# Attention, expert layer and gated layer on one core: the gated layer's token chunks 408, 408 and 272 wide

## The chip, the cores and the metric

One core of one Trainium2 chip runs the whole kernel. The metric is the time of one execution on the device, in microseconds (us). Three executions of the kernel before took 453.52, 452.41 and 452.5 us, median 452.5 us.

## What is computed

Four batches of 1088 tokens go through three layers, all in float32:

```python
k_p, q_p = phi(k), phi(q)                  # phi: outer product of two 8-wide projections, per head
x = (q_p @ (k_p.T @ v)) / (q_p @ k_p.sum(0) + 1e-6)          # 1. attention, 4 heads of 32
xk, xr = mix(x, x_prev, mu_k), mix(x, x_prev, mu_r)
x = sigmoid(xr @ w_r) * (relu(xk @ w_k)**2 @ w_v)             # 2. expert layer, 128 -> 1024 -> 128
u, v = split(relu(x @ w_in))                                  # 3. gated layer, 128 -> 2 x 512
v_n = (v - mean(v)) / sqrt(var(v) + 1e-6)
v_s = w_spatial @ v_n + b_spatial          # 1088 x 1088 over the tokens, per batch
out = (u * v_s) @ w_out                                       # 512 -> 128
```

In what follows "the first part" is attention and the expert layer, which the kernel runs interleaved, and "the second layer" is the gated layer.

## The kernel before, in words

**Precision.** A float32 product is made of three matmuls on rounded halves (`mm3`, line 128: low x high, high x high, high x low). `copy` (line 133, ScalarE) makes a high half, `low` (line 137, VectorE or GpSimd) the low half.

**The first part.** Tokens are cut into the chunks of `CH` (line 22: 384, 384, 320), twelve over the four batches. `features`, `k_sum`, `q_turn`, `q_num` and `q_out` (lines 204 to 301) are attention; `up`, `sqsplit` and `down` (lines 354 to 410) step through 96 slices of the expert layer. A table `todo`, filled by `plan` (line 937), says after which slice each other piece of work is put into the program. Small buffers of this part have tags of their own: `bs0`, `bs1`, `sab` (line 215), `va0`, `va1` (line 198), `kb0`, `kb1` (line 243), `Sbd` (line 848), `de0`, `de1` (line 279). A tag is one buffer; a new tile of a tag waits until the old one is no longer used.

**The second layer, batch 0.** `spatial` (line 548) makes one unit: 128 of the 512 channels (d) times one chunk of output tokens (c). It has 3 matmuls for u, 24 for the token product (8 blocks of 128 tokens), 2 for the tail of 64 tokens and the bias, and 3 for the output product (`put_out`, line 573): 32 matmuls as wide as the chunk. The twelve units run in the order of `ORD0` (line 64); the first four, chunks 0 and 1 of d = 0 and 1, are put among the last slices of the first part (`ES`, line 49, planned at line 1010), the last four have chunk 2. The token matrix is loaded by chunk (`wload`, line 431) into two staging buffers `st0` and `st1` and split by `wconv` (line 439).

**The second layer, batches 1 to 3.** `group` (line 694) takes two of the four channel blocks, so there are six groups. Chunks 0 and 1, both 384 wide, and the two halves of 1024 tokens make a 2 x 2 block product, which is done with seven half-size products instead of eight (`prod`, line 709; sums of the token matrix in `sums`, line 639, kept at the places of `CHOME`, line 79; sums of v in `build`, line 680). A product is 4 blocks x 3 = 12 matmuls, so a group has 84 of them, 384 wide. Chunk 2, 320 wide, is done plainly: four calls of `plain` (line 714) of 12 matmuls each, 48 a group. Around these, each of a group's two channel blocks has for each chunk 3 matmuls for u (`pre`, line 698), 2 for the tail (`tmm`, line 719) and 3 for the output product.

**The order.** The program is traced in this order, and a scheduler that simulates the engines' times then orders the instructions of each engine. `behind` (line 896) pins some of them.

```python
CH = ((0, 384), (384, 384), (768, 320))                                     # line 22
ORD0 = ((0, 0), (1, 0), (0, 1), (1, 1), (2, 0), (3, 0), (2, 1), (3, 1), (3, 2), (0, 2), (1, 2), (2, 2))
```

Of the kernel before, what the change touches and what calls it, by code (L numbers as in the profile page):

```python
# [78 lines left out]
CHOME = {(1, 2): ("tt", 0), (3, 2): ("tt", 1), (1, 3): ("tt", 2), (3, 3): ("tt", 3), (1, 0): ("tt", 4), (3, 0): ("x0",),  # L79
# [5 lines left out]
def attn_moe_gmlp(ctx: ExitStack, tc: tile.TileContext, qT, kT, va, st, wk, wv, wr, win, wout,  # L85
# [118 lines left out]
    def features(src, c, dst, pb=4, eng=None, early=False):  # L204
        wide = bank(pb)
        ab = wide[:, :192].rearrange("p (t h r) -> p t h r", t=3, h=NH)
        for t in range(3):
            TE.matmul(wide[:, 64 * t:64 * t + 128], lhsT=src[:, cut(c, t, CH[c][0])], rhs=Sbd, start=True, stop=True)  # L208
        if eng is None:
            bs = sb(rot("bs0", "bs1"), [128, 3, NH, 8])  # L210
            copy(bs, ab[:, :, :, 8:16])
            a_ = ab[:, :, :, 0:8].rearrange("p t h i -> p (t h) i")
            b_ = bs.rearrange("p t h j -> p (t h) j")
        else:
            sab = sb(m(2 + c) if early else "sab", [128, 3, NH, 16])
# [52 lines left out]
    def q_num(i):  # L268
# [10 lines left out]
        den = sb(rot("de0", "de1"), [128, 3, NH])  # L279
# [138 lines left out]
    def wplace(k, c):  # L418
        if c < 2:
            t = WTAGS[NT * c + k]  # L420
            return (t, 0), (t, CMAX)
        return (WTAGS[2 * k], 2 * CMAX), (WTAGS[2 * k + 1], 2 * CMAX)

    def wtile(k, c):
        n = CH[c][1]
# [5 lines left out]
    def wload(k, c):  # L431
        o, n = CH[c]
# [6 lines left out]
    def wconv():  # L439
        k, c, src = pending_raw.pop(0)  # L440
        done.add((k, c))
        o, n = CH[c]
# [105 lines left out]
    def spatial(b, d, c, fill, early=False):  # L548
# [6 lines left out]
        o, n = CH[c]  # L555
# [17 lines left out]
    def put_out(b, d, c, g, early=False):  # L573
        o, n = CH[c]
# [21 lines left out]
    def ctile(n, k):  # L596
# [5 lines left out]
        if (n, k) not in ct:  # L602
            tags = CHOME[n, k]
            if tags[0] == "tt":
                if "c" not in xv:
                    xv["c"] = sb("tt", [128, 5, 2, CMAX], F32R)
                ct[n, k] = tuple(xv["c"][:, tags[1], x] for x in range(2))
            elif len(tags) == 1:
                t = sb(tags[0], [128, 2, CMAX], F32R)
                ct[n, k] = t[:, 0], t[:, 1]  # L610
            else:
                ct[n, k] = tuple(sb(t, [128, CMAX], F32R) for t in tags)
        return ct[n, k]

    def wraw(dst, n, k):
        o = CH[n % 10 - 1][0]
        r = 128 * (k + HALF * (n // 10 - 1))
        nc.sync.dma_start(out=dst, in_=wT[r:r + 128, o:o + CMAX])
# [75 lines left out]
    def group(b, p):  # L694
# [3 lines left out]
        def pre(d, c, relu=False):  # L698
            o, n = CH[c]
# [24 lines left out]
        def snap(acc):  # L724
            a = sb(rot(m(8), m(9), m(10), m(11)), [128, CMAX])
# [37 lines left out]
        X = bank(0)[:, :CMAX]  # L763
# [7 lines left out]
        Y = bank(1)[:, :CMAX]  # L771
# [7 lines left out]
        Y = bank(1)[:, :CMAX]  # L779
# [13 lines left out]
        Z = bank(6)[:, :CMAX]  # L793
# [15 lines left out]
        if last_group:  # L809
            while gout:  # L810
                flush()
            ob = sb(rot(m(6), m(7)), [128, CMAX])
            for h in range(2):
                cs = slice(CMAX // 2 * h, CMAX // 2 * h + CMAX // 2)
# [4 lines left out]
            nc.sync.dma_start(out=out[:, b * S + CMAX:b * S + 2 * CMAX], in_=ob)  # L819
# [341 lines left out]
```

## Time and profile before

| what | value |
|---|---|
| median of three executions | 452.5 us (452.41 to 453.52) |
| the profiled execution | 452.46 us |
| its span (first to last instruction) | 450.7 us |
| TensorE busy in the span | 440.8 us, 98% |
| VectorE, ScalarE, GpSimd busy | 297.5, 270.4, 223.2 us |
| granted TensorE clock | 1.0 of full speed in all of the span |

The profile follows one execution. PE is TensorE, PEld its weight loads, DVE VectorE, ACT ScalarE, POOL GpSimd, SP the queue that issues the transfers. The duration given for a matmul holds its way through the array, so durations of neighbours overlap; what a matmul costs in a full stream is the distance from its start to the start of the next. L131 is line 131 of the kernel. A row of the timeline merges equal instructions that follow each other ("x12").

### The profile page before, as it was taken

The numbers are of one execution on the slowest core, as the hardware profiler recorded it, in microseconds if no ns is written. First come the engines' busy times: TensorE is split into PE (matmuls) and PEld (weight loads), VectorE is DVE, ScalarE is ACT, GpSimd is POOL, SyncE is SP. The second block draws the span as 40 slices with busy tenths as digits, with TensorE's granted clock in tenths as the row PEclk, the third lists the DMA queues.
The fourth block names the chain that finished last, engine by engine and source line by source line (L and its number), as shares of the span: only waits on it lengthen the run. The fifth ranks groups of instructions, "written<-read, shape, count | busy, mean of one in ns | idle before, by whom it ended". The sixth has DMA issues, their size and how long they took to land.

```text
span 450.7 us, 7621 instructions
## 1 busy us (share of the span) xinstructions
PE 440.8 (98%) x2691; PEld 420.4 (93%) x2691; DVE 297.5 (66%) x531; ACT 270.4 (60%) x629; POOL 223.2 (50%) x271
## 2 busy tenths in 40 slices
PE   8899999999999999999999999999999999999997
PEld 7897989989998988899999999999999999999996
DVE  5995777779864986566587797862755951734513
ACT  2595888998977898767446664334545434533322
POOL 2166477496744585868222426544435534335220
PEclk9999999999999999999999999999999999999999
DMA  7981100011100030033238422313022232010001
GB/s 232 369 297 49 51 0 2 2 52 54 27 2 0 22 120 19 19 87 113 59 117 256 131 63 93 118 54 110 15 85 93 72 110 69 19 41 25 0 2 49
DMA packets 30950, 34.92 MB, mean 77 GB/s; under 512 B 2816, under 2 KB 26432, under 8 KB 30912
## 3 DMA queue, kind: packets, MB, share of 16 engines
q1 hardware_dynamic: 30768, 34.43, 23.8%
q8 instruction: 21, 0.34, 0.3%
q14 instruction: 17, 0.14, 0.1%
q10 hardware_dynamic: 144, 0.01, 0.0%
HBM read 25.91 MB, written 8.52 MB: 76 GB/s over the span
## 4 chain that ended last, share of the span: by engine, by line
PE 84%; DVE 6%; DMA 3%; ACT 3%; POOL 1%; issue 1%; SPq 1%; ACTq 0%; DVEq 0%
PE p L131 67%; PE p L406 5%; PE p L276 3%; PE p L239 2%; PE p L208 2%; DMA w<-in_wk_dram 1%; PE p L260 1%; PE p L722 1%; PE p L721 1%; DMA st<-in_wT_dram 1%; DVE w L148 1%; DVE w L147 1%; PE p L294 1%; ACT m L362 1%; DVE mx L319 1%
## 5 line engine op out<-in xcount | busy, mean ns | idle before, releaser
L131 PE MATMUL p<-m,k 128*128 128x384 f32 (+1 forms) x288 | 65.5, 349 | 0.0
L131 PE MATMUL p<-w,k 128*128 128x384 f32 (+1 forms) x360 | 63.8, 323 | 0.0
L131 PEld LDWEIGHTS p<-w,k 128*128 128x128 f32 x360 | 59.2, 188 | 0.3
L621 DVE TENSOR_TENSOR m<-p,m 128x384 f32<-128x384 f32 (+2 forms) x37 | 18.6, 520 | 57.0 <-PE p L722 56.1
L134 ACT ACTIVATE m<-m 128x384 fp32r<-128x384 f32 (+2 forms) x49 | 24.6, 502 | 45.9 <-DVE m L735 25.6
L131 PEld LDWEIGHTS p<-m,k 128*128 128x128 f32 x288 | 48.2, 189 | 4.1
L137 POOL TENSOR_TENSOR k<-VR,k 128x512 fp32r<-128x512 f32 x25 | 34.0, 1364 | 33.4 <-ACT k L134 28.6
L362 ACT ACTIVATE m<-p 128x384 f32<-128x384 f32 (+1 forms) x96 | 43.1, 468 | 8.2 <-PE p L131 6.4
L137 DVE TENSOR_TENSOR m<-m,m 128x384 fp32r<-128x384 f32 (+1 forms) x48 | 34.3, 715 | 11.2 <-ACT m L134 8.8
L131 PE MATMUL p<-w,n1H 128*128 128x384 f32 (+1 forms) x192 | 41.1, 326 | 0.0
L365 POOL TENSOR_TENSOR m<-m 128x384 f32<-128x384 f32 (+1 forms) x35 | 30.0, 859 | 21.5 <-ACT m L362 21.0
L137 DVE TENSOR_TENSOR w<-m,w 128x384 fp32r<-128x384 f32 (+1 forms) x35 | 26.0, 746 | 15.4 <-POOL m L365 11.4
L131 PE MATMUL p<-w,n1L 128*128 128x384 f32 (+1 forms) x168 | 34.8, 324 | 0.9 <-POOL n1L L137 0.9
L134 ACT ACTIVATE m<-p 128x384 f32<-128x384 f32 (+1 forms) x36 | 17.1, 482 | 30.0 <-PE p L131 21.7
L137 POOL TENSOR_TENSOR n1H<-VR,n1H 128x512 fp32r<-128x512 f32 x12 | 15.5, 1293 | 37.1 <-ACT n1H L134 26.4
L406 PE MATMUL p<-w,wvT 128*128 128x384 f32 (+1 forms) x86 | 33.4, 470 | 0.0
L131 PEld LDWEIGHTS p<-w,n1H 128*128 128x128 f32 x192 | 32.6, 188 | 0.5
L500 POOL TENSOR_SCALAR rs<-mv 128x1 f32<-128x1 f32 x34 | 8.8, 260 | 43.3 <-DVE mv L499 42.4
L131 PEld LDWEIGHTS p<-w,n1L 128*128 128x128 f32 x168 | 28.5, 188 | 1.4 <-POOL n1L L137 1.2
L504 DVE TENSOR_SCALAR VR<-VR,mv,rs 128x512 f32<-128x512 f32 x24 | 20.5, 855 | 12.6 <-POOL rs L501 12.3
L134 ACT ACTIVATE k<-VR 128x512 fp32r<-128x512 f32 x25 | 15.7, 630 | 21.4 <-PE p L131 17.1
L131 PE MATMUL p<-w,xs1H 128*128 128x384 f32 (+1 forms) x90 | 26.9, 338 | 0.0
(288 smaller groups left out, 1212.6 us busy)
## 6 DMA issues: line engine op xcount, KB each, us to landing
vd<-VR SPq DMA_DIRECT2D x24, 256.0 KB, 2.0
VR<-vd SPq DMA_DIRECT2D x24, 256.0 KB, 2.9
st<-in_wT_dram SPq DMA_DIRECT2D x16, 192.0 KB, 2.4
w<-in_kT_dram SPq DMA_DIRECT2D x8, 192.0 KB, 4.4
w<-in_qT_dram SPq DMA_DIRECT2D x8, 192.0 KB, 4.0
VR<-in_wT_dram SPq DMA_DIRECT2D x8, 192.0 KB, 2.6
out_dram<-m SPq DMA_DIRECT2D x8, 192.0 KB, 2.1
m<-in_wT_dram SPq DMA_DIRECT2D x8, 192.0 KB, 4.5
```

Source lines behind the costliest of these rows:

```text
L131: TE.matmul(out_ap, lhsT=l, rhs=r, start=first and n == 0, stop=last and n == 2, skip_group_check=skip)
L134: return SE.activation(out=dst, in_=src, func=AF.Copy)
L137: return eng.tensor_tensor(out=L, in0=src, in1=H.bitcast(F32), op=ALU.subtract)
L208: TE.matmul(wide[:, 64 * t:64 * t + 128], lhsT=src[:, cut(c, t, CH[c][0])], rhs=Sbd, start=True, stop=True)
L239: TE.matmul(kv[:, w * g:w * g + w], lhsT=kp, rhs=vt if wide else vt[:, VP * g:VP * g + VP], start=(t == 0), stop=(t == NT - 1))
L276: nd_pe[0] = TE.matmul(o.rearrange("p h c -> p (h c)"), lhsT=qt[g][:, cut(c, t)], rhs=kb[:, g], start=not wide or g == 0, stop=not wide or ...
L362: SE.activation(out=r, in_=hk, func=AF.Relu)
L365: anchor[2] = GE.tensor_tensor(out=sq, in0=r, in1=r, op=ALU.mult)
L406: TE.matmul(vvs[i], lhsT=wvT[:, f // 2], rhs=hls.pop(g), start=f == 0, stop=f == NF - 1)
L500: GE.tensor_scalar(out=rs, in0=mv[:, 1:2], scalar1=1e-6, scalar2=None, op0=ALU.add)
L504: VE.tensor_scalar(out=v, in0=r, scalar1=mv[:, 0:1], scalar2=rs, op0=ALU.subtract, op1=ALU.mult)
L621: return eng.tensor_tensor(out=o, in0=a, in1=b_, op=op)
```

## The change

The second layer gets its own chunks, `C2`: 408, 408 and 272 tokens. The first part keeps `CH`. All widths, offsets and places of the second layer follow (`wplace`, `wtile`, `wload`, `wconv`, `spatial`, `put_out`, `ctile`, `wraw`, `stage`, `sums_load`, `tail_load`, `group`). One combination of the token matrix, (1, 0), moves out of the tile `tt`, which then holds four instead of five. The small buffers of the first part become slices of one tile `misc`, whose tag later holds that combination. Its core:

```diff
+MISC = {"bs0": 96, "bs1": 96, "sab": 192, "va0": 132, "va1": 132, "kb0": 264, "kb1": 132, "Sbd": 128, "de0": 12, "de1": 12}
 CMAX = 384
+CM2 = 408
+C2 = ((0, 408), (408, 408), (816, 272))
...
-CHOME = {(1, 2): ("tt", 0), (3, 2): ("tt", 1), (1, 3): ("tt", 2), (3, 3): ("tt", 3), (1, 0): ("tt", 4), (3, 0): ("x0",),
+CHOME = {(1, 2): ("tt", 0), (3, 2): ("tt", 1), (1, 3): ("tt", 2), (3, 3): ("tt", 3), (1, 0): ("misc",), (3, 0): ("x0",),
...
+    misc = sb("misc", [128, sum(MISC.values())])
+    small = {}
+    for name, n in MISC.items():
+        o = sum(x.shape[1] for x in small.values())
+        small[name] = misc[:, o:o + n]
...
-        t2 = sb(rot("va0", "va1"), [128, NH, HD + 1])
+        t2 = small[rot("va0", "va1")].rearrange("p (h c) -> p h c", h=NH)
...
-            bs = sb(rot("bs0", "bs1"), [128, 3, NH, 8])
+            bs = small[rot("bs0", "bs1")].rearrange("p (t h r) -> p t h r", t=3, h=NH)
...
-            kb = sb(f"kb{b % 2}", [128, 2 * nh, HD + 1])
+            kb = small[f"kb{b % 2}"].rearrange("p (h c) -> p h c", c=HD + 1)
...
-            return (t, 0), (t, CMAX)
-        return (WTAGS[2 * k], 2 * CMAX), (WTAGS[2 * k + 1], 2 * CMAX)
+            return (t, 0), (t, CM2)
+        return (WTAGS[2 * k], 2 * CM2), (WTAGS[2 * k + 1], 2 * CM2)
...
     def wload(k, c):
-        o, n = CH[c]
+        o, n = C2[c]
...
-                    xv["c"] = sb("tt", [128, 5, 2, CMAX], F32R)
+                    xv["c"] = sb("tt", [128, 4, 2, CM2], F32R)
...
-        X = bank(0)[:, :CMAX]
+        X = bank(0)[:, :CM2]
...
             for h in range(2):
-                cs = slice(CMAX // 2 * h, CMAX // 2 * h + CMAX // 2)
+                cs = slice(CM2 // 2 * h, CM2 // 2 * h + CM2 // 2)
```

## Rows read from the trace of the kernel before

**Rows 1.** The page: span, and busy time of TensorE.

```profile
span 450.7 us, 7621 instructions
...
PE 440.8 (98%) x2691; PEld 420.4 (93%) x2691; DVE 297.5 (66%) x531; ACT 270.4 (60%) x629; POOL 223.2 (50%) x271
```

**Rows 2.** Stretches: busy us of each engine, then clock, DMA share, GB/s.

```profile
160.00:204.20 44.20, 42.57 (x236) 39.11 (x234) 29.41 (x44) 34.75 (x87) 30.02 (x33) 1.00 0.21 62
204.20:445.80 241.60, 241.60 (x1440) 238.24 (x1439) 145.62 (x262) 112.04 (x241) 101.52 (x122) 1.00 0.24 77
445.80:450.70 4.90, 1.57 (x8) 0.87 (x6) 0.88 (x3) 0.98 (x2) 0.00 (x0) 1.00 0.22 80
```

**Rows 3.** Waits of TensorE: us in total, times, longest.

```profile
PE p L131 <- POOL n1L L137: 0.9, 1, 0.9
...
PE p L406 <- ACT m L382: 0.7, 1, 0.7
```

**Rows 4.** Timeline of TensorE in a group: start, us, instructions.

```profile
333.78 2.26 PE L131 MATMUL p<-w,k 128*128 128x384 f32 x12
335.88 0.34 PE L721 MATMUL p<-m,T 128*128 128x384 f32 x1
...
337.19 1.91 PE L131 MATMUL p<-w,k 128*128 128x320 f32 x12
338.94 0.39 PE L131 MATMUL p<-winL,xs1H 128*128 128x512 f32 x1
...
339.62 1.93 PE L131 MATMUL p<-w,k 128*128 128x320 f32 x12
```

**Rows 5.** Timeline of TensorE in the first part, narrow matmuls.

```profile
132.51 0.83 PE L239 MATMUL p<-xs0L,n0H 128*128 128x66 f32 x6
133.18 0.83 PE L239 MATMUL p<-xs0L,n0L 128*128 128x66 f32 x6
```

**Rows 6.** Chain of waits, 160 to 206 us: start, us, what.

```profile
190.97 2.58 DMA st<-in_btail_dram
...
197.08 2.56 DMA st<-in_wT_dram
...
200.69 2.16 DMA st<-in_wT_dram
...
203.25 0.46 ACT m L382
...
203.76 0.81 PE p L406 x2
```

**Rows 7.** Transfers: count, KB each, median us from issue to landing.

```profile
st<-in_wT_dram SPq DMA_DIRECT2D x16, 192.0 KB, 2.4
...
out_dram<-m SPq DMA_DIRECT2D x8, 192.0 KB, 2.1
...
st<-in_wT_dram SPq DMA_DIRECT2D x8, 160.0 KB, 2.2
...
out_dram<-m SPq DMA_DIRECT2D x4, 160.0 KB, 1.8
...
va<-in_va_dram SPq DMA_DIRECT2D x4, 66.0 KB, 5.5
```

**Rows 8.** VectorE by shape: count, busy us, mean ns, idle before.

```profile
L621 DVE TENSOR_TENSOR m<-p,m 128x384 f32<-128x384 f32 x23 | 12.2, 550 | 34.5 <-PE p L722 34.5
...
L621 DVE TENSOR_TENSOR m<-p,m 128x320 f32<-128x320 f32 x12 | 5.9, 489 | 22.4 <-PE p L722 21.6 <-ACT m L134 0.7
...
L282 DVE TENSOR_TENSOR VR<-p,de 128x384 f32<-128x384 f32 x12 | 6.7, 556 | 0.3
```

**Rows 9.** Timeline from 446 us: the last matmuls.

```profile
446.48 0.90 PE L817 MATMUL p<-m,idn 128*128 128x192 f32 x4
```

**Rows 10.** Timeline of GpSimd, 276 to 290 us: one low half.

```profile
279.26 1.49 POOL L137 TENSOR_TENSOR k<-VR,k 128x512 fp32r<-128x512 f32 x1
```

**Rows 11.** Timeline of TensorE, 255 to 292 us: its first use.

```profile
281.77 0.69 PE L131 MATMUL p<-x,k 128*128 128x384 f32 x3
```

More of the change, by code (lines that the diff above doesn't have):

```diff
@@ L214, in features @@
         else:
-            sab = sb(m(2 + c) if early else "sab", [128, 3, NH, 16])
+            sab = sb(m(2 + c), [128, 192]) if early else small["sab"]
+            sab = sab.rearrange("p (t h r) -> p t h r", t=3, h=NH)
             copy(sab, ab)
@@ L278, in q_num @@
         xm = qst[i] = vr(rot(4, 5), CMAX).rearrange("p (t h c) -> p t h c", t=3, h=NH)
-        den = sb(rot("de0", "de1"), [128, 3, NH])
+        den = small[rot("de0", "de1")].rearrange("p (t h) -> p t h", t=3)
         VE.tensor_scalar(out=den, in0=nd[:, :, :, HD], scalar1=1e-6, scalar2=None, op0=ALU.add)
@@ L420, in wplace @@
             t = WTAGS[NT * c + k]
-            return (t, 0), (t, CMAX)
-        return (WTAGS[2 * k], 2 * CMAX), (WTAGS[2 * k + 1], 2 * CMAX)
+            return (t, 0), (t, CM2)
+        return (WTAGS[2 * k], 2 * CM2), (WTAGS[2 * k + 1], 2 * CM2)
     def wtile(k, c):
-        n = CH[c][1]
+        n = C2[c][1]
         for t, _ in wplace(k, c):
@@ L441, in wconv @@
         done.add((k, c))
-        o, n = CH[c]
+        o, n = C2[c]
         H, L = wtile(k, c)
@@ L554, in spatial @@
         xH, xL = xsp[b]
-        o, n = CH[c]
+        o, n = C2[c]
         cs, ds = slice(o, o + n), slice(128 * d, 128 * d + 128)
@@ L573, in put_out @@
     def put_out(b, d, c, g, early=False):
-        o, n = CH[c]
+        o, n = C2[c]
         ds = slice(128 * d, 128 * d + 128)
@@ L605, in ctile @@
                 if "c" not in xv:
-                    xv["c"] = sb("tt", [128, 5, 2, CMAX], F32R)
+                    xv["c"] = sb("tt", [128, 4, 2, CM2], F32R)
                 ct[n, k] = tuple(xv["c"][:, tags[1], x] for x in range(2))
             elif len(tags) == 1:
-                t = sb(tags[0], [128, 2, CMAX], F32R)
+                t = sb(tags[0], [128, 2, CM2], F32R)
                 ct[n, k] = t[:, 0], t[:, 1]
             else:
-                ct[n, k] = tuple(sb(t, [128, CMAX], F32R) for t in tags)
+                ct[n, k] = tuple(sb(t, [128, CM2], F32R) for t in tags)
         return ct[n, k]
     def wraw(dst, n, k):
-        o = CH[n % 10 - 1][0]
+        o = C2[n % 10 - 1][0]
         r = 128 * (k + HALF * (n // 10 - 1))
-        nc.sync.dma_start(out=dst, in_=wT[r:r + 128, o:o + CMAX])
+        nc.sync.dma_start(out=dst, in_=wT[r:r + 128, o:o + CM2])
     def tt(eng, o, a, b_, op):
@@ L625, in stage @@
     def stage(j):
-        return VR[:, j, :CMAX]
+        return VR[:, j, :CM2]
     def sums_load(k, *ns):
@@ L630, in sums_load @@
             h = WHOME[k, n]
-            raws[k, n] = stage(h) if isinstance(h, int) else sb(h, [128, CMAX])
+            raws[k, n] = stage(h) if isinstance(h, int) else sb(h, [128, CM2])
             wraw(raws[k, n], n, k)
@@ L660, in tail_load @@
         for x, c in ((10, 0), (11, 1)):
-            raws[NK, c] = sb(m(x), [128, CMAX])
-            nc.sync.dma_start(out=raws[NK, c], in_=btail[:, CH[c][0]:CH[c][0] + CMAX])
+            raws[NK, c] = sb(m(x), [128, CM2])
+            nc.sync.dma_start(out=raws[NK, c], in_=btail[:, C2[c][0]:C2[c][0] + CM2])
     def tail_sums():
@@ L698, in pre @@
         def pre(d, c, relu=False):
-            o, n = CH[c]
+            o, n = C2[c]
             w, cs = slice(128 * d, 128 * d + 128), slice(o, o + n)
@@ L724, in snap @@
         def snap(acc):
-            a = sb(rot(m(8), m(9), m(10), m(11)), [128, CMAX])
+            a = sb(rot(m(8), m(9), m(10), m(11)), [128, CM2])
             copy(a, acc)
@@ L748, in third @@
                 tu[0] = pre(q, 2, True)
-                tu[1] = bank(6)[:, :CH[2][1]]
+                tu[1] = bank(6)[:, :C2[2][1]]
             plain(tu[1], a, not second)
@@ L770, in group @@
         yield
-        Y = bank(1)[:, :CMAX]
+        Y = bank(1)[:, :CM2]
         prod(Y, 12, 21, True)
@@ L778, in group @@
         yield
-        Y = bank(1)[:, :CMAX]
+        Y = bank(1)[:, :CM2]
         prod(Y, 22, 4, True)
@@ L792, in group @@
         yield
-        Z = bank(6)[:, :CMAX]
+        Z = bank(6)[:, :CM2]
         prod(Z, 1, 1, True)
@@ L818, in group @@
             copy(ob, po[1])
-            nc.sync.dma_start(out=out[:, b * S + CMAX:b * S + 2 * CMAX], in_=ob)
+            nc.sync.dma_start(out=out[:, b * S + CM2:b * S + 2 * CM2], in_=ob)
         else:
@@ L847, in attn_moe_gmlp @@
     split64(rawS, 16, None, Sl, Ss)
-    Sb = sb("Sbd", [128, 2 * NH, 16])
+    Sb = small["Sbd"].rearrange("p (h r) -> p h r", r=16)
     VE.tensor_tensor(out=Sb, in0=Ss.unsqueeze(1).to_broadcast([128, 2 * NH, 16]),
                      in1=mk[:, 0:2 * NH].unsqueeze(2).to_broadcast([128, 2 * NH, 16]), op=ALU.mult)
-    Sbd = flat(Sb)
+    Sbd = small["Sbd"]
     for t in T2s:
```

2 lines of the change are left out of this document (1 added, 1 removed).

## The prediction, made before the changed kernel ran

> **What bounds the kernel now.** I read the page's list of busy times first: TensorE is busy 440.8 us of a span of 450.7 us [rows 1]. An average hides where the other 10 us lie, so the second view was the busy time by stretch [rows 2]. From 204.2 to 445.8 us, which is all of the second layer but its early units and its end, TensorE is busy without a gap: 241.60 of 241.60 us, while VectorE has 145.6 us of work, ScalarE 112.0 and GpSimd 101.5. Here a TensorE nanosecond saved is a nanosecond of time. From 160 to 204.2 us TensorE misses 1.6 us, and the list of its waits names both gaps [rows 3]: 0.9 us for a low half of the normalised v (tile n1L), 0.7 us for the square of the last expert slices. The last 4.9 us are the end: short DVE, PE and ACT steps and the store.
>
> The third view is the timeline inside a group, for the distance between matmul starts, since durations overlap. Twelve matmuls of 384 columns take 335.88 - 333.78 = 2.10 us, 175 ns each; twelve of 320 columns take 338.94 - 337.19 = 1.75 us, about 147 ns; three of 512 take 339.62 - 338.94 = 0.68 us, 227 ns (rounded rows) [rows 4]. Between 320 and 384 columns that is 28 ns for 64 columns, 0.44 ns a column, with some 7 ns that don't depend on the width. The granted clock is 1.00, the full 2.4 GHz, in each of these stretches [rows 2].
>
> **The columns.** No matmul is added or removed; 24 columns go onto those of chunks 0 and 1, and 48 come off those of chunk 2. By the slope a wide one becomes 24 x 0.4375 = 10.5 ns longer (185.5 ns) and a narrow one 21 ns shorter (126 ns). Everything that is done once per chunk cancels: a channel block of batch 0 has 2 x 32 wide and 32 narrow ones, 64 x 10.5 = 32 x 21; in the groups the u, tail and output matmuls are 2 x 8 wide and 8 narrow, which cancels too. What doesn't cancel is the token product of batches 1 to 3: chunks 0 and 1 are done with seven products instead of eight. A group has 84 wide matmuls, +882 ns, and 48 narrow ones, -1008 ns: -126 ns, and for six groups **-0.76 us**. This is the difference of two sums of about 10 us (952 wide matmuls at +10.5, 512 narrow ones at -21), so it hangs on the 126 ns.
>
> The trace has no 272-column matmul. Its bounds are the 147 ns of 320 columns (narrowing gives nothing) and the floor of the narrowest pairs, 66 columns at (133.18 - 132.51) / 6 = 112 ns [rows 5]. I take 126 ns, by the slope, since it stands above that floor; one nanosecond more on 512 matmuls costs 0.5 us.
>
> The Trainium skill ("TensorE: Matmul & The Clock Gate", Back-to-back issue gap) puts the gap of a warm matmul at its columns / 2.4 + 2.5 ns, 115.8 ns for 272 columns; the rows lie above it (175 ns against 162.5 for 384). By its slope, 10 and 20 ns, the groups would save 0.72 us instead.
>
> **The early units.** Four of batch 0's units, all of chunks 0 and 1, run before 204 us; each has 32 matmuls x 10.5 = 0.34 us more, 1.34 us together, and the four chunk-2 units at the end of batch 0 get 2.69 us shorter. So 1.34 us of TensorE work moves from the stretch without gaps into the one with gaps. Where a gap swallows it, it is free. The first unit comes before the 0.9 us gap and can hide 0.34 us there; the other three bring 1.0 us in front of the 0.7 us gap and could fill it. The best is thus -1.04 us. The other end is zero, or a loss if the gaps' own causes become later: the second gap hangs on a chain without TensorE, three loads into the staging buffers (2.58, 2.56, 2.16 us) with the ACT copies behind them, and the square that PE waits for stands in ACT's queue behind a copy that waits for such a load [rows 6]. A load of 192 KB lands after 2.4 us and one of 160 KB after 2.2 us [rows 7], so 204 KB costs some 0.1 us more and 136 KB 0.15 us less; the chain has one of the first and two of the second, nearly nothing. The scheduler will lay these instructions out anew, so I take half of the best, **-0.5 us**.
>
> The Trainium skill ("DMA: Bandwidth & Descriptors", How a descriptor splits into AXI transactions) speaks against the change here: a row that doesn't start at a multiple of 256 B fetches bytes that it doesn't use, and 1632 and 3264 B are no such multiples where 1536 and 3072 were. By its count a chunk-2 row would still cost the 40 beats of a 320-column one, so the two loads stay at 2.2 us and the sum would be some 0.3 us higher, 451.7 us. No run here shows it so far.
>
> **The end.** After the last product the path gets wider: the two half-width DVE steps by 12 columns each, at (550 - 489) / 64 = 0.95 ns a column [rows 8] some 0.02 us, the low half and the ACT copy by 24 columns, 0.04 us; the four records of the last matmul [rows 9] by some 10 ns each, 0.04 us; the store, 192 KB in 2.1 us and 160 KB in 1.8 us [rows 7], by 0.1 us. Together **+0.2 us**. Bounds: zero, and 0.3 us.
>
> **At nothing.** Sums, snaps and joins of the groups get 24 columns wider, 0.02 to 0.03 us each on DVE and ACT; what hides them is their distance to use. One of the shorter ones is a low half that GpSimd ends at 279.26 + 1.49 = 280.75 us [rows 10] and TensorE first uses at 281.77 us [rows 11]: 1.0 us, and the matmuls in that gap get longer as well. If this cover went, six groups would pay tenths of a microsecond each. The shared tile `misc` holds the same bytes, and a slice needs to wait only for users of the same slice. That is how the tile VR already works: PE, ACT and DVE use its slices at once, and the twelve DVE writes of L282 into it have 0.3 us of idle before them in all [rows 8]. Nothing, then; the bound above is a rival. The weight conversions of chunks 0 and 1 get 6% longer, in the first part, where DVE and POOL have room [rows 2].
>
> **The sum.** The profiled execution took 452.46 us, 1.76 us more than its span, and stands 0.04 us below the median of the three runs. 452.46 - 0.76 - 0.5 + 0.2 = **451.4 us**. A measurement of this kernel can tell about 0.3%, 1.36 us, from no change, so faster means below 451.1 us and slower above 453.8 us: the forecast itself is "no difference that can be told", close to the edge.
>
> **The rivals.**
> (a) Forecast, 450.9 to 452.1 us: chance 0.43, a quarter of it below the edge.
> (b) Both gaps take all they can: 452.46 - 0.76 - 1.04 + 0.2 = 450.9 us or a little less. For it speaks that the moved work lies just in front of the gaps and needs nothing from the chain behind them; against it, that the order on PE's queue is planned anew. 0.25, faster.
> (c) The column saving is there, but the new layout gives it back and no gap closes: 452.46 - 0.76 + 0.2 + 0.4 = 452.3 us. The change then doesn't do what it says. 0.10, no difference.
> (d) Slower: the wait in ACT's queue at 203 us. If the new order puts one more staging load ahead of the square for which PE waits, PE waits one load longer, 2.4 us: 452.46 - 0.56 + 2.4 = 454.3 us. It decides from an added wait of 1.9 us on. For it: three loads already follow one another there [rows 6]. Against it: chunk 2's loads are smaller and PE has 1 us more to do. 0.12, a third of it inside the 0.3%.
> (e) The narrow matmuls don't follow the slope. At 130 ns they cost 2 us more (453.4 us), at 147 ns 10.8 us more (462 us). For it: 126 ns is only 14 ns above the floor. Against it: slope and floor are both steady. 0.06. The Trainium skill ("TensorE: Matmul & The Clock Gate", LDWEIGHTS and Back-to-back issue gap) has such a rule: both the load and the matmul set the spacing, and a load of 128 columns takes 128 / 1.2 = 107 ns. The 112 ns of 66 columns agree with it, and by it 272 columns would still be above the load.
> (f) The shared tile is waited for as a whole. A write to one buffer would then wait for loads into another, up to 5.5 us for a `va` load [rows 7], twice or so on the path: 455 to 462 us. VR speaks against it. 0.04.
>
> **The numbers.** Faster: (b) and a quarter of (a), 0.36. Slower: two thirds of (d), half of (e), all of (f), 0.15. Within 0.3%: 0.49. The range goes from 450.5 us, (b) with the end at nothing and a slightly steeper slope, to 453.2 us, which takes in (c), the mild third of (d) and (e) up to 129 ns; above it some 0.15 is left out, below it little.
>
> **What would show it.** In the trace after: 408 columns at 185 to 186 ns and 272 columns at 126 ns (128 ns would undo the saving, 112 ns would add 7 us to it); TensorE still without a gap from about 204 us to the end, that stretch shorter by some 2.1 us (1.34 moved, 0.76 saved); the early units longer by 1.34 us, with the n1L gap near 0.6 us and the gap in front of L406 gone or small; a wait of a `bs`, `sab` or `kb` write for another buffer's load would show (f). The prediction is wrong if TensorE gets new gaps of more than 2 us before 204 us, or if the first 160 us, which I take as unchanged, move by a microsecond.

## The result, and the profile after

The changed kernel takes **455.04 us** (median of five executions, 454.5 to 455.74) against 452.5 us before: ratio 1.0059, 95% interval 1.0047 to 1.0071. That is 2.5 us slower, outside the range forecast (450.5 to 453.2 us) and on the other side of no change. The profiled execution took 455.57 us. In what follows line numbers are those of the changed kernel, 9 or 10 higher than before (L131 is now L140, L137 is L146, L621 is L631).

The page of the changed kernel, its span and TensorE's busy time, the lines that answer to [rows 1]:

```profile
span 453.8 us, 7614 instructions
...
PE 442.7 (98%) x2691; PEld 420.4 (93%) x2691; DVE 299.5 (66%) x531; ACT 270.2 (60%) x629; POOL 223.6 (49%) x271
```

Its stretches (busy us of TensorE, its loads, VectorE, ScalarE, GpSimd, then clock, DMA share, GB/s), which answer to [rows 2]; the third runs from unit 6 of batch 0 (units counted from 0) into the first group of batch 1:

```profile
160.00:206.40 46.40, 45.44 (x246) 42.02 (x245) 29.43 (x46) 34.62 (x86) 30.44 (x33) 1.00 0.20 56
206.40:229.30 22.90, 22.90 (x122) 22.19 (x121) 13.65 (x27) 13.68 (x34) 12.19 (x16) 1.00 0.31 93
229.30:277.00 47.70, 45.94 (x298) 43.58 (x296) 39.71 (x75) 26.28 (x59) 17.63 (x27) 1.00 0.45 142
277.00:448.60 171.60, 170.92 (x1014) 168.75 (x1015) 93.41 (x162) 72.27 (x149) 71.63 (x80) 1.00 0.18 57
```

About the same stretch of the kernel before:

```profile
229.10:276.90 47.80, 47.80 (x300) 46.86 (x299) 38.97 (x80) 28.04 (x62) 17.74 (x26) 1.00 0.46 144
```

TensorE, without a gap there before, now misses 1.8 us of it and 0.7 us just behind it (a matmul's row holds its way through the array, so the distances between starts grow by more). VectorE is busy 82% of it before (38.97 of 47.8 us), the average of the whole second layer being 60% [rows 2]. That is close to the most that any 47.8 us of the second layer reach (39.5 us, 83%, from 244 us on): here VectorE has little to spare. TensorE's waits name VectorE (us in all, times, longest); the n1L gap of [rows 3] is 0.2 us shorter and the one in front of the last expert slices (L406 before) is gone:

```profile
PE p L140 <- DVE m L631: 1.2, 1, 1.2
PE p L140 <- DVE m L146: 0.9, 2, 0.6
PE p L140 <- POOL n1L L146: 0.7, 1, 0.7
```

Measured between the same matmuls in both traces, the span grows by 3.1 us as follows: from 52 us in the first part to the end of batch 0's last unit, +0.24 us (+1.82 to the end of unit 3, +0.89 from there to unit 7, -2.47 to unit 11); the **first group 41.82 to 45.39 us, +3.57**; the five other groups -0.60 together (-0.16, -0.11, -0.09, -0.14, -0.10); the start and the end -0.1 together. The mark at a group's end is the first tail matmul of the next group. So the whole loss lies in one group of six, and it is as large as TensorE's gaps between 256 and 278 us (distances of matmul starts over the usual ones: 3.7 us).

**Where VectorE's time went.** Its timeline in the changed kernel (start, us, engine, line, operation, idle before and what ended it):

```profile
251.73 0.58 DVE L631 TENSOR_TENSOR m<-m,m 128x408 f32<-128x408 f32 x1
...
252.72 0.43 DVE L580 TENSOR_TENSOR m<-p,m 128x272 f32<-128x272 f32 x1
253.07 1.32 DVE L631 TENSOR_TENSOR m<-m,m 128x408 f32<-128x408 f32 x1
256.71 1.39 DVE L146 TENSOR_TENSOR mx<-m,m 128x408 fp32r<-128x408 f32 x1 [2.32 <-ACT m L143]
...
258.38 1.67 DVE L631 TENSOR_TENSOR m<-m,VR 128x408 f32<-128x408 f32 x1
...
261.31 1.65 DVE L631 TENSOR_TENSOR VR<-m,VR 128x408 f32<-128x408 f32 x1
...
272.33 1.25 DVE L679 CAST m<-m 1x408 fp32r<-1x408 f32 x1
...
274.44 0.51 DVE L514 TENSOR_SCALAR VR<-VR,mv,rs 128x512 f32<-128x512 f32 x1
275.69 1.49 DVE L514 TENSOR_SCALAR VR<-VR,mv,rs 128x512 f32<-128x512 f32 x1 [0.74 <-POOL rs L511]
277.11 0.92 DVE L631 TENSOR_TENSOR m<-p,m 128x272 f32<-128x272 f32 x2
```

GpSimd's timeline there, low halves of combinations of v (line 702, `build`); the first four rows are the first group's first four:

```profile
252.48 1.48 POOL L146 TENSOR_TENSOR n1H<-VR,n1H 128x512 fp32r<-128x512 f32 x1 [2.83 <-issue]
...
256.38 1.28 POOL L146 TENSOR_TENSOR n1L<-VR,n1L 128x512 fp32r<-128x512 f32 x1 [1.66 <-ACT n1L L143]
258.31 1.29 POOL L146 TENSOR_TENSOR k<-VR,k 128x512 fp32r<-128x512 f32 x1 [0.65 <-ACT k L143]
261.22 1.29 POOL L146 TENSOR_TENSOR k<-VR,k 128x512 fp32r<-128x512 f32 x1 [1.62 <-ACT k L143]
...
271.38 1.97 POOL L146 TENSOR_TENSOR n1H<-VR,n1H 128x512 fp32r<-128x512 f32 x1 [8.11 <-ACT n1H L143]
...
275.63 1.28 POOL L146 TENSOR_TENSOR k<-VR,k 128x512 fp32r<-128x512 f32 x1
```

Lay the two side by side. The VectorE step of 253.07 ends at 254.39, GpSimd's low half of 252.48 at 253.96; the next three pairs end at 258.10 and 257.66, 260.05 and 259.60, 262.96 and 262.51. Each VectorE step ends 0.43 to 0.45 us after GpSimd's instruction, whenever it began: it waits rather than runs slower. The cast of 272.33 and the step of 275.69 end 0.23 and 0.27 us after GpSimd's low halves of 271.38 and 275.63. The same add takes 0.58 us at 251.73. The step at 252.72, beside the same low half, takes its own 0.43 us; one of its inputs is in PSUM (`p`). The six long steps take 8.77 us; at their own durations (four of 0.58, 0.43 for the cast where nothing runs beside it, 0.51 at 274.44) they would take 3.26. **VectorE loses 5.5 us to GpSimd here**, 3.7 of them beside the first group's first four low halves. The Trainium skill ("SBUF — State Buffer", SBUF: two separate sides) has this as a rule: VectorE and GpSimd share a pair of ports as an exclusive lock; whichever starts first, a GpSimd instruction or a VectorE one with two SBUF inputs or in a two-port mode, holds it for the whole instruction, and the other blocks. The trace agrees in the order of the ends (0.43 to 0.45 us) and in the PSUM step, though a blocked step ends sooner behind GpSimd's than its own 0.58 us.

In the kernel before, VectorE:

```profile
254.35 0.56 DVE L137 TENSOR_TENSOR w<-m,w 128x384 fp32r<-128x384 f32 x1 [2.09 <-ACT w L134]
...
259.46 1.37 DVE L137 TENSOR_TENSOR st<-VR,st 128x384 fp32r<-128x384 f32 x1 [0.21 <-ACT st L134]
...
268.77 0.82 DVE L669 CAST m<-m 1x384 fp32r<-1x384 f32 x1
...
272.30 1.40 DVE L504 TENSOR_SCALAR VR<-VR,mv,rs 128x512 f32<-128x512 f32 x1
273.62 0.94 DVE L621 TENSOR_TENSOR m<-p,m 128x320 f32<-128x320 f32 x2
```

and GpSimd:

```profile
251.96 1.29 POOL L137 TENSOR_TENSOR n1H<-VR,n1H 128x512 fp32r<-128x512 f32 x1 [4.22 <-issue]
253.21 1.29 POOL L137 TENSOR_TENSOR n1L<-VR,n1L 128x512 fp32r<-128x512 f32 x1
...
257.27 3.14 POOL L137 TENSOR_TENSOR k<-VR,k 128x512 fp32r<-128x512 f32 x2 [2.03 <-issue]
```

Two of the four low halves fall into the 2.09 us in which VectorE waits for ScalarE anyway, and a third mostly beside a PSUM step and a pause. Three steps are long; they lose about 2.1 us (at 0.55, 0.4 and 0.55 of their own). 5.5 - 2.1 = 3.4 us, against the group's +3.57.

Why they no longer fall there is read from ScalarE. Changed kernel, then kernel before:

```profile
255.61 0.63 ACT L143 ACTIVATE n1L<-VR 128x512 fp32r<-128x512 f32 x1 [2.60 <-DMA VR<-vd]
256.15 0.53 ACT L143 ACTIVATE m<-m 128x408 fp32r<-128x408 f32 x1
```

```profile
252.47 0.63 ACT L134 ACTIVATE n1L<-VR 128x512 fp32r<-128x512 f32 x1 [0.64 <-DMA VR<-vd]
```

The copy that goes ahead of the second low half waits 2.60 us for its load instead of 0.64. Behind it in ScalarE's queue stands the copy for which VectorE waits (the 2.32 us at 256.71). The last store of batch 1's v goes out at 248.02 instead of 245.88 us and lands after 4.6 instead of 3.6 us; the reload, which waits for it, goes out at 252.69 instead of 249.50 us. The store is late since it is made during units 5 to 8, behind eight units that are 24 columns wider, while the first group begins at nearly the same time (0.24 us later by the sum above, less the 0.15 us that the start is shorter).

What that lateness costs is seen at 274 us. TensorE before, in the first group:

```profile
274.50 0.52 PE L131 MATMUL p<-xrH,n1H 128*128 128x384 f32 x2
274.85 0.31 PE L131 MATMUL p<-m,woL 128*128 128x320 f32 x1
```

and after, with rows for the width of 272 as well:

```profile
259.36 1.67 PE L140 MATMUL p<-w,n1L 128*128 128x272 f32 x12
260.86 0.29 PE L731 MATMUL p<-w,T 128*128 128x272 f32 x1
...
275.95 0.53 PE L140 MATMUL p<-xrH,n1H 128*128 128x408 f32 x2
277.68 0.61 PE L140 MATMUL p<-misc,n1L 128*128 128x408 f32 x2 [1.20 <-DVE m L631]
```

Before, VectorE's chunk-2 steps (273.62 + 0.94 = 274.56 us) were done 0.3 us ahead of TensorE's next matmul at 274.85. That was the whole margin there. After, they begin at 277.11, and TensorE stands still.

### The profile page after: what moved, and what is told of

The parts are those of the page before. It is cut to its first block, busy times and chain, and to the rows that moved or that the text cites. A ratio compares the mean times of both kernels' runs of the same rounds, so it can differ in the third digit from the quotient of the medians.

```text
span 453.8 us, 7614 instructions
## 1 busy us (share of the span) xinstructions
PE 442.7 (98%) x2691; PEld 420.4 (93%) x2691; DVE 299.5 (66%) x531; ACT 270.2 (60%) x629; POOL 223.6 (49%) x271
## 4 chain that ended last, share of the span: by engine, by line
PE 68%; DVE 16%; POOL 4%; DMA 4%; issue 3%; ACT 3%; SPq 1%; ACTq 0%; POOLq 0%; DVEq 0%
PE p L140 55%; PE p L416 3%; DVE w L146 2%; PE p L249 2%; PE p L286 2%; DMA w<-in_wk_dram 1%; PE p L217 1%; PE p L270 1%; PE p L732 1%; PE p L731 1%; DVE m L146 1%; DVE w L157 1%; DMA vd<-VR 1%; DVE m L631 1%; DVE w L156 1%
## 5 line engine op out<-in xcount | busy, mean ns | idle before, releaser
L140 PE MATMUL p<-m,k 128*128 128x384 f32 (+1 forms) x288 | 66.2, 351 | 0.0
L140 PE MATMUL p<-w,k 128*128 128x408 f32 (+1 forms) x360 | 62.5, 320 | 0.0
L140 PEld LDWEIGHTS p<-w,k 128*128 128x128 f32 x360 | 58.0, 188 | 0.4
L631 DVE TENSOR_TENSOR m<-p,m 128x408 f32<-128x408 f32 (+2 forms) x37 | 18.5, 518 | 57.0 <-PE p L732 57.0
L140 PEld LDWEIGHTS p<-m,k 128*128 128x128 f32 x288 | 48.3, 189 | 4.5 <-ACT m L372 0.5
L146 POOL TENSOR_TENSOR k<-VR,k 128x512 fp32r<-128x512 f32 x25 | 33.2, 1330 | 34.8 <-ACT k L143 31.7
L143 ACT ACTIVATE m<-m 128x408 fp32r<-128x408 f32 (+3 forms) x49 | 24.5, 502 | 40.1 <-DVE m L745 21.5
L372 ACT ACTIVATE m<-p 128x384 f32<-128x384 f32 (+1 forms) x96 | 43.0, 467 | 8.6 <-PE p L140 8.2
L146 DVE TENSOR_TENSOR m<-m,m 128x408 fp32r<-128x408 f32 (+2 forms) x48 | 33.2, 694 | 12.7 <-ACT m L143 9.3
L140 PE MATMUL p<-w,n1H 128*128 128x408 f32 (+1 forms) x192 | 39.3, 321 | 0.1
L143 ACT ACTIVATE m<-p 128x408 f32<-128x408 f32 (+1 forms) x36 | 17.5, 495 | 33.9 <-PE p L140 23.1
L140 PE MATMUL p<-w,n1L 128*128 128x408 f32 (+1 forms) x168 | 34.3, 320 | 0.7 <-POOL n1L L146 0.7
L146 POOL TENSOR_TENSOR n1H<-VR,n1H 128x512 fp32r<-128x512 f32 x12 | 16.4, 1363 | 37.1 <-ACT n1H L143 34.2
L146 DVE TENSOR_TENSOR w<-m,w 128x384 fp32r<-128x384 f32 (+2 forms) x35 | 25.9, 739 | 13.2 <-POOL m L375 10.8
L140 PEld LDWEIGHTS p<-w,n1H 128*128 128x128 f32 x192 | 31.7, 188 | 0.6 <-ACT n1H L143 0.4
L140 PEld LDWEIGHTS p<-w,n1L 128*128 128x128 f32 x168 | 28.0, 188 | 1.3 <-POOL n1L L146 1.1
L140 PE MATMUL p<-w,xs1H 128*128 128x384 f32 (+1 forms) x90 | 26.7, 340 | 0.0
```

The costliest lines, as they stand in the source:

```text
L140: TE.matmul(out_ap, lhsT=l, rhs=r, start=first and n == 0, stop=last and n == 2, skip_group_check=skip)
L143: return SE.activation(out=dst, in_=src, func=AF.Copy)
L146: return eng.tensor_tensor(out=L, in0=src, in1=H.bitcast(F32), op=ALU.subtract)
L372: SE.activation(out=r, in_=hk, func=AF.Relu)
L631: return eng.tensor_tensor(out=o, in0=a, in1=b_, op=op)
```

## The experiments

All times are medians; each ratio is to the kernel before, run on the same chip in the same session (452.08 to 452.30 us). Beside it stands the first two groups' time in the profiled execution, 73.92 us before and 77.33 after (41.82 + 32.10, 45.39 + 31.94), taken together because some edits move work from one into the other.

**The shared tile alone** (e2_misc): the changed kernel with the old widths.

```diff
-CM2 = 408
-C2 = ((0, 408), (408, 408), (816, 272))
+CM2 = 384
+C2 = ((0, 384), (384, 384), (768, 320))
```

> The shared tile and the moved combination alone: chunks 384, 384 and 320 as before. Theory A: the first group finds its v blocks as before; 452.0 to 453.2 us, no gap of TensorE between 255 and 285 us. Theory B: the loss is here, 454 to 455.5 us. Theory C: as A, 452.0 to 453.2 us.

451.23 us, ratio 0.998 (0.9971 to 0.9989): 0.85 us faster, below what any of the theories expected, two groups 73.68 us. The tile and the moved combination don't cause the loss; it comes with the widths. Widths without the tile weren't tried: the wider buffers need the room that the tile gives back.

**Half the shift** (e4_396): 396, 396 and 296 tokens.

```diff
-C2 = ((0, 408), (408, 408), (816, 272))
+C2 = ((0, 396), (396, 396), (792, 296))
```

> Half the change: chunks of 396, 396 and 296. Columns alone: 0.38 us saved. Theory E: the stretch of VectorE starts some 1.15 us later and hardly ends sooner, half the loss of the changed kernel, 453.2 to 454.0 us, with gaps of TensorE of some 1.5 to 2 us between 255 and 280 us. Theory A1 (a swap that is there or not): ScalarE's two copies stand in the order of the changed kernel here as well, so 454.3 to 455.2 us. Columns only: 452.0 us.

452.31 us, ratio 1.0001 (0.9986 to 1.0016), but executions from 451.25 to 453.93 us. The profiled one is the slowest: the load wait on ScalarE is 3.1 us there and the two groups take 75.37 us. That this width stands at the edge, and that late loads tip it, is a reading of this one trace.

**The load wait.** Four edits on ScalarE's wait of 2.60 us. First, `build` of the block in question later in the program (e6_build12), then v of batch 1 made a unit earlier (e1_vearly):

```diff
-            add(4, build, 1, 0, 1)
+            pass
...
+            build(1, 0, 1)
```

> The changed kernel with one thing moved: the copy and split of v's block 12 for the first group come after those of block 21 in the program, so that ScalarE does not stand in front of a load that lands late. Theory A (the last v tile of batch 1 and so the load of block 12 come some 2 us later against the first group; ScalarE waits 2.6 us for it at the head of its queue, VectorE loses 2.3 us behind it and TensorE then 3.8 us): the wait of ScalarE for that load shrinks below 1 us, TensorE's gaps between 255 and 280 us shrink from 3.8 us to below 1 us, time 451.2 to 452.5 us. Theory B (the shared tile and the moved combination cost the time): nothing changes, 454.5 to 455.5 us. Theory C (the 408-wide sums are simply too much work for VectorE there): VectorE stays late, 454 to 455.5 us.

454.73 us, ratio 1.0065 (1.0049 to 1.0082). The scheduler put the copy back almost where it was (load wait 2.2 us, the same gaps), so this run decides nothing.

```diff
-        for n, j in enumerate({5: (0, 1), 6: (2, 3), 7: (4, 5), 8: (6, 7)}.get(u, ())):
+        for n, j in enumerate({5: (0, 1, 2), 6: (3, 4, 5), 7: (6, 7)}.get(u, ())):
...
+        if u == 8:
+            add(2, v_rest)
         if u == 9:
-            add(2, v_rest)
```

> The changed kernel with the eight v tiles of batch 1 spread over units 5 to 7 (three, three, two) instead of 5 to 8, so that the last one is stored some 6 us earlier. Theory A: the loads of v's blocks land in time, ScalarE does not wait for one, TensorE's gaps between 255 and 280 us shrink to below 1 us, time 451.0 to 452.5 us. Theory B: no change, 454.5 to 455.5 us. Theory C: the same work of VectorE is only moved forward, where it also has the sums to do; gaps remain, 453.5 to 455.5 us.

454.05 us, ratio 1.0048 (1.0033 to 1.0063), two groups 75.59 us. The load wait is gone, and so are the gaps at 256 to 258 us; 0.6 us at 262 and 1.46 us at 275 us are left. The profiled execution gets 1.7 us back in the two groups, the ratios 0.5 us, with intervals that overlap (1.0047 to 1.0071 for the changed kernel). The wait is at most a part of the loss.

Third, the kernel before with its last v tile later (e5_vlate), which should bring the wait about:

```diff
-        for n, j in enumerate({5: (0, 1), 6: (2, 3), 7: (4, 5), 8: (6, 7)}.get(u, ())):
+        for n, j in enumerate({5: (0, 1), 6: (2, 3), 7: (4, 5), 8: (6,), 9: (7,)}.get(u, ())):
```

> The kernel before (384, 384, 320, separate small buffers) with the last v tile of batch 1 made in unit 9 instead of unit 8, some 3 us later. Theory A: it shows the stall of the changed kernel without any of its widths: ScalarE waits 2 us or more for the load of block 12, VectorE behind it, TensorE 2 us or more between 255 and 285 us; 454.5 to 457 us. Theories B and C: VectorE's work and the tiles are as before; 452.3 to 453.2 us.

452.09 us, ratio 0.9997 (0.9987 to 1.0006). The wait on ScalarE stayed at 0.7 us, against theory A. The last store did go out later against the first group, 7.2 us ahead of the last unit's tail matmul instead of 9.6 (7.6 in the changed kernel). But it landed after 2.2 us instead of 3.6 (4.6), so that the reload went out 4.9 us ahead of that matmul instead of 6.0 (2.9). A later store alone doesn't bring the wait; how long it takes to land counts too. Fourth, ScalarE's copy pinned behind the one that VectorE waits for (e9_act):

```diff
-        copy(H, src)
+        raws["copy", n, k] = copy(H, src)
...
-            add(4, build, 1, 0, 1)
+            add(4, lambda: behind([raws["copy", 2, 0]], build, 1, 0, 1))
```

> The changed kernel with one order pinned on ScalarE: the copy of v's block 12 of the first group (which waits for a load) is issued behind the copy of the combination (2, 0), as it stands in the kernel before; in the changed kernel the two are the other way round. Theory A1 (this swap costs: VectorE waits 2.3 us for the copy of (2, 0) that stands behind the waiting one, and is late from there on): VectorE's wait at 254 to 257 us goes, TensorE's gaps from 255 to 265 us (2.4 us) shrink below 1 us, time 452.2 to 453.3 us, or 451.3 us if the gap at 276 us goes with them. Theory A2 (the load itself is late, whatever stands behind it): gaps stay, 454.5 to 455.5 us. Theory C (too much VectorE work with 408 columns): 454 to 455.5 us.

454.31 us, ratio 1.0047 (1.0032 to 1.0062), two groups 76.39 us: 0.9 us back there and 0.5 us by the ratios, again with intervals that overlap, and the 1.4 us gap at 275 us stays.

**TensorE's order at 276 us.** In the changed kernel two matmuls of one product (`misc,n1L`) stand ahead of another product; e8_pin puts them behind it, e10_both does that and e9's pin, e11_vpin that and e1's earlier v.

```diff
...
-        tmm(Y, e, ctile(5, NK))
+        y_last = tmm(Y, e, ctile(5, NK))
...
-        prod(Z, 1, 1, True)
+        behind([y_last] if early else [], prod, Z, 1, 1, True)
```

> The changed kernel with one order pinned on TensorE in the first group: the matmuls of product 1 are issued behind the last of product 22 x 4, as in the kernel before; in the changed kernel two of them stand ahead of it and wait for bank 6, which VectorE has yet to read. Theory D (TensorE stands 1.4 us before an instruction that it need not do yet): the gap at 276 us goes, the others stay, 453.2 to 453.9 us. Rival: the bank is needed anyway and the gap only moves to the next instruction that waits for VectorE, 454.5 to 455.3 us.

> Both pins together. If the two orders are the whole loss: gaps of TensorE after 255 us below 0.5 us, time 451.0 to 452.0 us, which is below the kernel before by the columns saved. If VectorE is late by its own work: 453 us or more.

> The changed kernel with the v tiles of batch 1 earlier (units 5 to 7) and the pin on TensorE. The v tiles alone gave 454.05 us and left a gap of 1.46 us at 275 us and 0.6 us at 262 us. Theory D: the 1.46 us go, 452.4 to 453.0 us. Rival as in the run with that pin alone: 453.8 to 454.3 us.

455.42, 454.77 and 454.37 us; ratios 1.0065 (1.0047 to 1.0083), 1.0062 (1.0047 to 1.0077) and 1.0053 (1.0038 to 1.0068). The gap goes to the next instruction (TensorE waits 1.6 us for a ScalarE copy behind the same VectorE steps). The order on TensorE is not the cause: VectorE is late whatever TensorE does first.

**Less VectorE work in the stretch.** Batch 2's v tiles one step later (e13_v2), and two chunk-1 units put behind two chunk-2 units in batch 0 (e15_ord).

```diff
-V2 = 3
+V2 = 4
...
+                    if b == 1:
+                        v_tile(b + 1, NK - 1, (3, 7))
+                        v_rest()
```

> The changed kernel with the v tiles of batch 2 one step later in the first group (the last of the eight at the start of the second group), so that statistics and normalisation of two tiles no longer stand in VectorE's queue ahead of the product of chunk 2 for which TensorE waits at 276 us. Theory E (from the end of unit 7 to that product VectorE is the bound: some 33 us of work in a chain with ScalarE in 40 us; the cover of TensorE's work there has become 3 us shorter): some 2.5 us of VectorE's work leave the stretch, the gap at 276 us (1.4 us) goes, time 453.0 to 453.9 us. Theory D (only two matmuls in a bad order): the gap stays or is found in another place, 454.5 to 455.3 us.

453.52 us, ratio 1.0028 (1.0016 to 1.0039), two groups 75.56 us: the gap at 276 us is gone, some 2 us of gaps at 255 to 264 us stay. Less VectorE work in the stretch gives back 1.4 us by the ratios, clear of noise.

```diff
-ORD0 = ((0, 0), (1, 0), (0, 1), (1, 1), (2, 0), (3, 0), (2, 1), (3, 1), (3, 2), (0, 2), (1, 2), (2, 2))
+ORD0 = ((0, 0), (1, 0), (0, 1), (1, 1), (2, 0), (3, 0), (3, 2), (0, 2), (2, 1), (3, 1), (1, 2), (2, 2))
```

> The changed kernel with two of the four chunk-2 units of batch 0 put ahead of the last two units of chunk 1: the last four units are 408, 408, 272, 272 wide instead of four times 272. Theory E: TensorE's work in VectorE's stretch is 1.9 us longer and what precedes it 1.9 us shorter; 452.8 to 454.0 us. Theory A1 (one swap on ScalarE) and theory D (one on TensorE): both orders are still swapped here, 454.5 to 455.3 us.

454.39 us, ratio 1.0044 (1.003 to 1.0057). In the profiled execution, one of its fastest (453.4 us), the two groups take 75.18 us, 2.2 less; over all executions, 453.21 to 455.52 us, it gains 0.7 us, with intervals that overlap. Where the others lose it wasn't seen.

**GpSimd's low halves on VectorE** (e12_lowdve, and e20_lowdve2 in another session): the first group's four low halves, 2.8 us more work for VectorE, and none left to wait for.

```diff
-        low(GE, t[:, 1], src, t[:, 0])
+        low(VE if (b, p) == (1, 0) and i < 4 else GE, t[:, 1], src, t[:, 0])
```

> The changed kernel with the four low halves of v of the first group made on VectorE instead of GpSimd. In the changed kernel the VectorE steps that run while GpSimd makes such a half take 1.3 to 1.7 us instead of 0.57 us. Theory P (this sharing is a large part of VectorE's lateness): four stretched steps of about 1.0 us each go and four of 0.7 us come, VectorE is 1 to 1.5 us earlier, time 453.5 to 454.3 us. Rival (VectorE's own work is the bound and the stretch only fills its waits): 2.8 us more work, 455 to 457 us.

> The changed kernel with the first group's first four low halves on VectorE, a second time, on the chip of the control runs: 451.88 us at first, ratio 0.9991 to the kernel before. Theory: again 451.3 to 452.6 us, so the whole loss of 2.5 us is the sharing between GpSimd and VectorE in the first group. Rival (the first result was chance of one session): above 453 us.

451.88 and 451.83 us, ratios 0.9991 (0.998 to 1.0002) and 0.9994 (0.9986 to 1.0003). The whole loss against the kernel before is gone, 2.9 us by the ratios (1.0059 to 0.9994) and more than theory P expected; the two groups take 73.46 us, where the forecast's column saving gives 73.92 - 0.25 = 73.67 and the tile alone, with the old widths, has 73.68. The stretch in e20_lowdve2, and VectorE's rows where it was held up before:

```profile
229.30:277.00 47.70, 47.70 (x315) 46.67 (x315) 41.49 (x86) 28.73 (x64) 18.04 (x24) 1.00 0.45 142
```

```profile
258.05 0.68 DVE L146 TENSOR_TENSOR k<-VR,k 128x512 fp32r<-128x512 f32 x1
258.65 0.58 DVE L631 TENSOR_TENSOR VR<-VR 128x408 f32<-128x408 f32 x1
```

TensorE has no gap, though VectorE does more. A low half costs VectorE 0.68 us here; on GpSimd it held VectorE up for 0.74 to 1.09 us. The load wait on ScalarE was still 2.0 us in e12: by itself it costs nothing there.

**Controls on the kernel before.** The same edit (e16_blow), and instead each of the four low halves made twice on GpSimd (e17_twice):

```diff
         low(GE, t[:, 1], src, t[:, 0])
+        if (b, p) == (1, 0) and i < 4:
+            low(GE, t[:, 1], src, t[:, 0])
```

> The kernel before, with the first group's first four low halves made by VectorE instead of GpSimd: the edit that took 3.2 us off the changed kernel. Theory (the changed order lets GpSimd's low halves fall onto VectorE's steps, which stretches them; in the kernel before they fall into VectorE's idle time): the kernel before has nothing to gain, so within 0.5 us of it, 451.8 to 452.8 us, no TensorE gap between 255 and 280 us. Rival (the low halves cost VectorE time in any order, or the edit simply gives a better order): 1 to 3 us less, 449.5 to 451.3 us.

451.93 us, ratio 0.9994 (0.9984 to 1.0003), no gap, two groups 73.91 us: nothing to gain there, so the edit is no better order in itself.

> The kernel before, with each of the first group's first four low halves made twice by GpSimd (5.2 us more GpSimd work, the result unchanged). Theory (VectorE is the bound from 229 to 277 us and GpSimd's low halves stretch its steps): the added halves fall onto VectorE steps, some of these take 1.2 to 1.7 us instead of 0.57, and TensorE gets gaps between 255 and 280 us: 0.7 to 3 us slower than the kernel before. Rival (GpSimd's work there costs VectorE nothing; only the order mattered): within 0.4 us, VectorE steps as before.

456.03 us, ratio 1.0089 (1.0072 to 1.0106), two groups 77.29 us: with old widths and old tiles, the loss is back, 3.4 us in the two groups as in the changed kernel, and more than expected in the time. VectorE in e17_twice:

```profile
255.31 1.65 DVE L621 TENSOR_TENSOR m<-m,VR 128x384 f32<-128x384 f32 x1
256.98 1.53 DVE L621 TENSOR_TENSOR VR<-VR 128x384 f32<-128x384 f32 x1
258.44 1.66 DVE L137 TENSOR_TENSOR n0L<-m,n0L 128x384 fp32r<-128x384 f32 x1
260.02 1.64 DVE L621 TENSOR_TENSOR VR<-m,VR 128x384 f32<-128x384 f32 x1
261.58 0.48 DVE L570 TENSOR_TENSOR m<-p,m 128x320 f32<-128x320 f32 x1
```

beside GpSimd

```profile
255.11 1.42 POOL L137 TENSOR_TENSOR n1H<-VR,n1H 128x512 fp32r<-128x512 f32 x1
256.50 1.60 POOL L137 TENSOR_TENSOR n1L<-VR,n1L 128x512 fp32r<-128x512 f32 x1
258.11 3.13 POOL L137 TENSOR_TENSOR k<-VR,k 128x512 fp32r<-128x512 f32 x2
```

and TensorE's longest wait:

```profile
PE p L131 <- DVE m L137: 1.7, 1, 1.7
```

VectorE now does one step per GpSimd instruction, each ending about 0.42 us after GpSimd's (256.96 after 256.53, 258.51 after 258.10). The cause is shown from both sides: with GpSimd's low halves taken away the changed kernel loses nothing against the kernel before, with more of them the kernel before loses as much.

**The milder width with that edit** (e19_396low).

```diff
-CM2 = 408
-C2 = ((0, 408), (408, 408), (816, 272))
+CM2 = 396
+C2 = ((0, 396), (396, 396), (792, 296))
...
-        low(GE, t[:, 1], src, t[:, 0])
+        low(VE if (b, p) == (1, 0) and i < 4 else GE, t[:, 1], src, t[:, 0])
```

> The changed kernel with chunks of 396, 396 and 296 tokens, and the first group's first four low halves on VectorE. Theory: half of the column saving (0.35 us) and no gaps in the first group, so 451.4 to 452.2 us, and no slow executions near 454 us, which the 396-wide kernel with the low halves on GpSimd had. Rival (its slow executions come from late loads): spread as before, median 452.3 us, some executions near 454 us.

451.91 us, ratio 0.9994 (0.9985 to 1.0003), executions from 451.33 to 453.02 us: the executions near 454 us are gone, and it is no better than 408. Its slowest, 453.02 us, which was profiled, has a load wait of 2.4 us and a TensorE gap of 0.3 us still. Of all versions only the shared tile alone beats both kernels by its interval, and by 0.2%: no version with wider chunks is faster than the tile without them.

## Why the prediction was wrong

- **The columns: the distances were right, the agreement of the saving is luck.** 272 columns start 125 ns apart (260.86 - 259.36 over 12), 408 columns 186 ns; forecast 126 and 185.5. Rival (e) falls. The five groups that nothing disturbs save 0.12 us each against the kernel before, as forecast (0.126). But the shared tile with the old widths (e2_misc) already saves 0.46 of the 0.50 us that groups two to five save: its wide and narrow matmuls start 174.5 and 146.3 ns apart instead of 175.2 and 146.8. Against these distances the widths are worth 84 x 11.5 - 48 x 20.9 = -37 ns in a group's products and 32 x 11.5 - 16 x 20.9 = +34 ns in its other matmuls: nothing. The prediction took the distances as the same wherever the tiles lie. What the widths would save with the tiles of the kernel before, no run shows.
- **The early units: half right.** The last expert slices' gap is gone and the n1L gap shorter, 0.9 us in all, but the stretch from the first part to the end of unit 11 came out at +0.24 us instead of -0.5. Some 0.6 us were lost in small steps before 160 us, which the prediction took as unchanged. About half of that is the same pattern again: at 103.77 us a VectorE low half takes 1.22 us beside GpSimd's of 103.61 (0.48 us before, when it came ahead of GpSimd's), the step of L420 starts behind it, and TensorE waits 0.2 us for that at 105.50, where it didn't before.
- **The shared tile, the end.** The tile alone costs nothing (e2_misc), so rival (f) falls; that it gains 0.85 us was not forecast. The end is longer by 0.05 to 0.14 us, by the mark from which it is measured, inside its bounds of zero and 0.3.
- **The staging loads.** 136 KB land after 2.1 us, 160 KB took 2.2; 204 KB after 2.4, like 192 KB [rows 7]. The rule on the start of rows that the prediction cites from the Trainium skill ("DMA: Bandwidth & Descriptors", How a descriptor splits into AXI transactions), by which the narrow load would have stayed at 2.2 us, shows no cost that these medians, 0.1 us apart, could tell. Rival (d), a load more in ScalarE's queue at 203 us, didn't come.
- **The step that failed is "At nothing"**: sums, snaps and joins were costed at nothing because one low half was made 1.0 us before its use [rows 10, 11]. In its place the first group alone lost 3.57 us, with VectorE losing 3.4 us more than before to GpSimd's low halves; the tenths of a microsecond in each of six groups, which the prediction gave as the price of lost cover, came in none. The prediction asked of each piece how much wider it gets, 0.02 to 0.03 us. It didn't ask what VectorE and GpSimd do at the same moment. The row for it was in the trace before: the step of 1.37 us at 259.46, of a kind that takes 0.55. The two rows that stood for the cover aren't a pair either: `k` names two buffers, and the matmul of 281.77 belongs to the product with combination 3, whose low half GpSimd had begun at 272.13 us. The low half of 279.26 is for the product that begins at 285.44, over 4 us behind its end. And both lie behind the tight place at 274 us, where the margin was 0.3 us. The row of the kernel before:

```profile
285.44 2.26 PE L131 MATMUL p<-w,k 128*128 128x384 f32 x12
```

- **What seems to have led there** is the moved work: 1.34 us were put in front of the gaps and booked as a gain for TensorE. In fact eight of batch 0's units got wider ahead of the first group, 2.7 us, and four narrower right before it, 2.5 us. TensorE breaks even; what hangs on the early units (batch 1's v) comes later, its last store by 2.1 us and the reload by 3.2, against a group that begins at nearly the same time. No rival held this: (d) looked for the wait at 203 us, 50 us too early, and on ScalarE.

That GpSimd's low halves hold VectorE up, and that this is the loss, is shown (e12_lowdve, e20_lowdve2, e17_twice, with e16_blow as control). That the later v is what moved them onto VectorE's steps is read from the traces and not shown: earlier v gave back 0.5 us by the ratios, within the noise, and a later store in the kernel before (e5_vlate) landed sooner and brought no wait.

## What to carry to other kernels

A busy share tells neither where an engine is short nor what it loses to a neighbour: before costing an edit at nothing, look for the stretch where the covering engine is fullest, and in it for instructions that take twice their usual time. Moving work from behind to ahead of a point is not neutral when its sum is zero, for whatever is issued by the moved work arrives later. When a change needs a new layout, run the layout alone: here it had most of what looked like the change's saving. Where VectorE is tight, a GpSimd instruction beside it can cost it more than doing that work itself: 0.74 to 1.09 us here against 0.68.

## What the runs showed of the hardware

- VectorE steps with both inputs in SBUF that begin during a GpSimd low half end 0.41 to 0.45 us after it for 384 and 408 columns, the `tensor_scalar` of line 514 0.27 us and the cast of line 679 0.23 us after it; steps with one PSUM input (0.43 us at 252.72, 0.48 us at 261.58 in e17_twice) are untouched. GpSimd's low half can be the longer one too: 1.97 us instead of 1.28 at 271.38, where a VectorE step had begun 0.3 us earlier. With GpSimd back to back, VectorE got in one step per GpSimd instruction (e17_twice).
- The same matmuls run at slightly different distances with tiles in other places: with the shared tile and the old widths 174.5 ns for 384 columns and 146.3 for 320, against 175.2 and 146.8 before, but 232.8 against 230.9 for 512 (means of the last five groups). Why stays open; on some 850 matmuls the first two are worth 0.5 us.
